# Another order for the first 900 of 2,700 tasks of a recurrence and an MLP on one core

## The chip, the cores and the metric

The kernel runs on one core of a Trainium2 chip. The core has five engines with a queue each: TensorE (PE, matrix products, with weight loads shown apart as PEld), VectorE (DVE), ScalarE (ACT), GpSimd (POOL) and SyncE (SP), which here issues all transfers between main memory and the core. An engine works through its queue strictly in order; engines wait for one another by semaphores. Products are written to PSUM, which VectorE and ScalarE read; everything else lies in SBUF, which GpSimd reads too. The metric is device time of one execution in microseconds (us), less is better.

## The reference

Two blocks in a row. The first is a recurrence over 768 time steps for 4 x 8 heads of width 40, with a 40 x 40 state per head; its output is laid out as 3,072 tokens of 320 channels and goes through an MLP with 2,048 hidden units:

```python
for t in range(S):
    y[:, :, t] = np.einsum('bhd,bhde->bhe', rt, state)
    Sa = np.einsum('bhde,bhe->bhd', state, at)
    state_decay = state * wt[:, :, None, :] - np.einsum('bhd,bhe->bhde', Sa, bt)
    state = state_decay + np.einsum('bhd,bhe->bhde', vt, kt)
...
x = np.ascontiguousarray(attn_out.transpose(0, 2, 1, 3)).reshape(B * S, H * D)
h = x @ w_in
g = h * (1.0 / (1.0 + np.exp(-1.702 * h)))
return (g @ w_out).astype(np.float32)
```

All inputs and outputs are float32.

## The kernel before

**Tiling.** Time is cut into 12 chunks of 64 steps. A unit i is one chunk c = i // 2 for one pair p = i % 2 of batches, with 16 heads; there are 24 units. Within a unit the recurrence is written as matrix products: scores of the 64 steps with one another (N from a and b, A from a and k, RV from r and v), a triangular inverse, and products with the state that the unit two before it left behind. Each chunk's result then passes through the MLP, 256 tokens at a time.

**The steps of a unit**, in the order of their chain:

- `logarithm` (L521) and `decay` (L538): the logarithm of w, its running sums by two products (`cum`, by time, and for the first four units `cumc`, by channel), and exponentials of them: FT and GT, wch, and G.
- `prep` (L613): ahT, bhT and khT are a, b and k times FT or GT; kh and bh are k and b by time, times G. The scores RV and A are products, masked while they are copied out.
- `inverse` (L662): the score N, then five levels. For the first four units (`plain_level`, L765) a level is a product on PE out of which one engine copies the next PT (called PV here) and VectorE transposes the next EX. Then come ES, Tc, the products Q and T21, and T. `preset` (L402) puts ones into a tile beforehand. In this text L0, L2, L4, L6 and L8 are the levels of unit 0, L1 to L9 (odd) those of unit 1, L10 to L18 (even) those of unit 2, and L11 to L19 (odd) those of unit 3.
- `solve` (L844): from unit 2 on the state is scaled (zr), turned (zT) and read (rz); B0 and B1 are products and sums, X is T times B, M is X masked, y is a product of RV, kh, M and bh. Out of y come the new state zraw and the unit's output, which `decayed` (L956) multiplies by FT into x. `part_with` (L967) stores x in main memory, and `get_back` (L973) loads it transposed as xT.
- `mlp` (L983): once both units of a chunk are in xT, 40 tasks `up`, four of GELU, 16 of `down`, and the stores.

A number behind a name is the unit's: N0 is the score N of unit 0, x1 the output of unit 1. In the profile, tiles go by the names in the code: EX<-ps_level is the transpose of a level, PT<-ps_level its copy.

**The weights** come as 64-bit pieces: eight of 1,280 columns, each loaded in four quarters (`weight`, L431), then treated by ScalarE (rebased), VectorE (bounded, shifted, rounded) and GpSimd (joined). Raw pieces go to few places, so that piece 5 is loaded where piece 0 was and has to wait until GpSimd has joined piece 0.

**The order.** `Plan.add` (L65) collects 2,700 tasks with what each reads, writes and needs room for; buffers have one to four slots (L280), so that for instance the load of b2 waits until N0 has read b0. The order is written out by hand, as one text, ORDER (L107), and `Plan.listed` (L89) reads it:

```python
e = next(e for e in ENGINES if ENGINES[e] in one)
n, bank = one.split(ENGINES[e])
t = self.tasks[int(n)]
...
t.engine, t.bank = e, int(bank or 0)
```

So `104a1` is task 104 on ScalarE (p is PE, a ScalarE, d VectorE, g GpSimd, s the transfers that SP issues), with the pair of PSUM banks 1 (there are four pairs, 0 to 3). The tasks are issued in that order (L1054), and so each engine's queue has it. Some tasks may run on either of two or three engines, and the letter decides. All products have line L300, as they go through one helper.

Of the kernel before, what the change touches and what calls it, by code (L numbers as in the profile page):

```python
# [111 lines left out]
279d 63s 280g 119p3 277s 171d1 36s 44s 120d3 343s 125d3 278g 124d3 29d 126p2 170a1 123a3 30d 172p1 122a3 127a2 121a 31d 128p2  # L112
54s 173a1 287a 288p0 289a0 129d2 32g 174d1 134p3 147s 37a 290d0 175p2 135d3 180a2 146s 178a2 275s 176d2 136p1 179a2 479s 38d
181a2 45s 39d 177a 282g 291d 91s 138a1 182p0 188p3 281d 183a0 186p2 139d 137a1 283p0 187a2 184p1 189a3 40d 276s 292p2 46a
284d0 41g 285p3 185d1 344s 148a 286d3 190p0 293a2 294d2 334p1 335p3 357a 140s 191d0 268g 336a3 315d 192p2 47d 337a1 348d 316p0
194a2 295p3 349d 61s 317a0 195g 60s 347s 358p1 296a3 62s 297d3 360d1 318a0 298p3 271a 361d 319p0 338g 300d3 196s 193a2 320a0
346s 355p2 385d 270s 48d 299a3 362p0 356d2 351g 301p3 363a0 364d0 350g 269s 141s 386p2 197s 302d3 365p0 387a2 352g 359a1 303d3
388a2 323p1 367d0 366a0 321p3 49d 324a1 304p2 322a3 478s 325d1 50g 353p0 309a2 470p3 354d0 209p1 307a2 210p1 310a2 305d2 211p1
308a2 272d 198p0 341a 199p0 72s 212p1 70s 64a 200p0 340s 368p2 52s 342d 339s 69s 201p0 369a2 202p0 370d2 203p0 471a 213p1 65d
214p1 389p2 66d 472a3 483g 204p0 390a2 560s 371p3 67d 306a 53s 215p1 71s 482s 216p1 372a3 217p1 476a 220p2 373d3 68g 218p1  # L120
221p2 477d 219a1 205p0 222p2 206p0 223p2 224p2 207p0 55a 311p3 225p2 79s 312d3 80s 226p2 208a0 58d 313p1 374p3 314d1 227p2 56d
379a3 228p2 229p2 57d 326p0 230a2 59g 393p1 327d0 378a3 391p2 394a1 375d3 231p0 558s 392d2 376a 232p0 233p0 395d1 559s 81s 73a
78s 234p0 480s 381p2 235p0 328p1 481s 382a2 74d 377a3 485d 380a3 236p0 75d 492a 242p2 486d 243p2 82a 76d 484d 77g 383p3 237p0
384d3 244p2 329d1 330d1 488p3 473d 238p0 531d 245p2 487g 246p2 489d3 85d 532p1 239p0 533a1 396p3 331d 332s 474s 475s 534a1
240p0 247p2 397d3 562s 241a0 535p1 83d 490p3 536a1 84d 398p0 572a 491d3 86g 550p1 555s 561s 253p3 399d0 551a 333s 400d0 254p3
401d 402s 554s 255p3 552a1 564d 493p0 705s 556a 567g 570p1 403s 494d0 248p2 563d 566g 249p2 495d0 498d 256p3 571d1 565g 250a2
496a0 251d2 252s 696p1 497g 557d 539p0 537p2 704s 257p3 538a2 540d0 258p3 553d 611d 697a 499d 573p2 784s 700s 259p3 576a2
574d2 710d 260p3 541d0 575d2 404p0 578d 261a3 577g 405p0 579d 698a1 568p2 711g 500p1 406p0 569d2 501a1 407p0 262d3 263s 708s
580p2 702a 502d1 408p0 582d2 409p0 503d 410p0 583d 504a 612p3 411p0 584g 613d3 412p0 614d3 413p0 505p1 709d 414a0 426p3 506d1
427p3 428p3 507d1 429p3 699d 581d2 430p3 615p1 785s 706s 701s 703d 431p3 616a1 585p0 432p3 508d 586a0 433p3 587d0 434p3 509a  # L130
588d 435p3 589d 448p2 436a3 510p1 590p0 511a1 449p2 592d0 591a0 512d1 415p3 513d 416p3 593d 514a 417p3 594g 418p3 515p0 419p3
516a0 517d0 595p1 518d 420p3 596a1 597d1 421p3 598d 422p3 519a 599d 423p3 424p3 520p0 425a3 437p1 521d0 438p1 523d0 522g 439p1
524d0 440p1 525d0 441p1 442p1 526d0 527p3 718p0 929s 528a3 443p1 719d0 787s 444p1 720d0 529p3 445p1 721d0 446p1 530d3 600p0
723d 447a1 542p3 722d 724g 603d0 605a0 619p1 604d0 543d3 450p2 620a1 606d0 544p3 621d1 601d0 602d 617p1 707s 546d3 451p2 618a1
783s 712d 547g 713d 607p0 725p1 608a0 452p2 609p0 453p2 548s 610d0 932s 454p2 727d1 726d1 622p0 728d 545d3 729a 775p1 455p2
623d0 780s 776a 549s 756d 730p3 624p0 456d2 457d2 731d3 458s 459p2 777a1 778g 732d3 786s 788g 781a 779s 626d0 460p2 625d0 627g
733d 795p1 835d 734a 461p2 735p3 791g 462p2 628s 736a3 796d1 737d3 716p0 792g 738d 463p2 782d 739g 1011s 920p1 757p3 925s
464p2 717d0 758a3 629s 759a3 790d 465p2 740p0 789d 466p2 741a0 742d0 921a 797p3 467d2 760p0 1008s 468d2 800a3 923d 652p2 469s
761d0 922a1 653p2 926a 930s 798d3 714p1 799d3 654p2 924s 802d 801g 655p2 934d 803a 656p2 836p0 657p2 715d1 658p2 659p2 837d0
762p3 838d0 927d 660p2 763a3 661p2 764p1 662a2 743d 630p0 744d 928s 631p0 632p0 765d1 804p3 766d1 633p0 805a3 806d3 634p0 807d  # L140
635p0 808a 745p2 636p0 748d2 637p0 749d2 839p1 933g 750d2 638p0 840a1 1009s 751d2 639p0 809p3 746d2 935g 640a0 641p1 810d3
642p1 793p2 747a 811d3 674p0 812d 794d2 813a 752p3 643p1 753a3 814p2 644p1 815a2 816d2 754p3 645p1 755d3 646p1 817d 647p1 818a
767p2 841p3 768d2 648p1 842a3 649p1 819p2 650p1 820a2 821d2 675p0 769p3 822d 651a1 823d 771d3 931s 770d3 772g 824p2 936d 676p0
827a2 828a2 942p1 829a2 677p0 1153s 830a2 937d 945a1 773s 663p3 825d2 664p3 943d1 1156s 826a 665p3 944d1 999p2 947d 946g 666p3
1000a 1004s 980d 940p1 948g 667p3 941d1 668p3 774s 669p3 670p3 831p1 671p3 1001a2 1002d 1003s 832d1 672p3 1005a 1013d 678p0
673a3 1006d 833p2 843p1 679p0 834d2 1007s 844d1 938p2 845d1 680p0 939d2 846p3 681p0 847d3 949p1 1012g 682d0 848p2 950a1 683d0
1014d 684s 685p3 849d2 1015g 1010s 850d2 1021p0 1016g 951d1 686p3 1024a0 1232s 851d 1235s 981p2 687p3 982a2 952d 852s 1022d0
983a2 953g 1144p1 1023d0 688p3 1026d 1145a 1149s 1025d 1027g 984p2 1059d 689p3 1154s 954p0 853s 985a2 1147g 690p3 1158d 1148s
955a0 956d0 986p2 1146a1 957d 1150a 691p3 958d 987a2 1151d 988p0 692p3 989a0 1152s 990d0 959p1 693a3 865p2 960a1 694d3 866p2
961d1 867p2 695s 962d 868p2 963d 1028p0 869p2 1029a0 1030d0 870p2 1031d 1157g 871p2 1159d 1032a 1060p3 872p2 873p2 1061a3  # L150
# [987 lines left out]
```

## Time and profile before

| what | us |
|---|---|
| median of 3 runs | 677.05 |
| lowest and highest run | 674.52, 680.86 |
| the profiled execution, from its first to its last instruction (span) | 676.5 |
| PE busy in it | 648.5 (96%) |
| VectorE, ScalarE, GpSimd busy | 444.6, 331.6, 175.3 |

The runs' times and the span are taken in different executions; the median lies 0.55 us above the span. A row of a list by time begins with its start and its length, in us from the start of the span, then engine, line, operation, the tiles written and read, shapes, and how many instructions it joins; in brackets stands how long the engine had been idle and what ended that. An SPq row is the issue of a transfer, not the transfer. Busy time of PE is modelled at the ends of products, so 96% busy does not mean 96% of its peak.

### The profile page before, as it was taken

The page shows a single profiled execution, that of the slowest core. Times are in us where ns is not written, and L with a number is a line of the kernel's source. Part 1 is how long each engine was busy: PE and PEld are TensorE (multiplying, and loading weights), DVE is VectorE, ACT ScalarE, POOL GpSimd, SP SyncE. Part 2 cuts the span into 40 slices and gives each one's busy share as a digit, 9 for nine tenths or more (in the row PEclk, how much of TensorE's full clock was granted, in tenths as well). Part 3 has the DMA queues.
Part 4 walks back from the last instruction along what each step waited for, and adds up shares of the span by engine and source line. Part 5 has one row for each costly group of instructions (what it writes and reads, how often), then busy time and mean ns, then how long its engine had stood idle before and what let it go on. Part 6 is the DMA issues. An engine that isn't in the chain of part 4 may idle for free.

```text
span 676.5 us, 42217 instructions
## 1 busy us (share of the span) xinstructions
PE 648.5 (96%) x19488; PEld 553.4 (82%) x19488; DVE 444.6 (66%) x908; ACT 331.6 (49%) x710; POOL 175.3 (26%) x204
## 2 busy tenths in 40 slices
PE   5768999999999999999999999999999999999997
PEld 5657887987998987788888888798888798798785
DVE  4786787777867667767776587768656766675001
ACT  4676755534564655664545445455454354252110
POOL 6344244224123123123123211322412421300000
PEclk9899999999999999999999999999999999999999
DMA  7983736315314314432404413513412411200200
GB/s 230 300 289 94 232 107 187 103 43 154 108 47 149 93 58 117 121 108 72 118 22 132 141 34 109 156 33 108 140 39 71 122 53 54 61 14 15 61 12 20
DMA packets 35313, 69.74 MB, mean 103 GB/s; under 512 B 5440, under 2 KB 14656, under 8 KB 35136
## 3 DMA queue, kind: packets, MB, share of 16 engines
q1 hardware_dynamic: 35136, 67.03, 32.6%
q8 instruction: 153, 2.51, 1.5%
q14 instruction: 24, 0.20, 0.1%
HBM read 59.15 MB, written 7.86 MB: 99 GB/s over the span
## 4 chain that ended last, share of the span: by engine, by line
PE 93%; DMA 2%; DVE 2%; issue 1%; ACT 1%; DVEq 0%; SPq 0%; ACTq 0%
PE ps_up L300 31%; PE ps_down L300 30%; PE ps_level L300 9%; PE ps_y L300 5%; PE ps_B L300 5%; PE ps_X L300 2%; PE ps_N L300 2%; PE ps_rz L300 2%; PE ps_RV L300 2%; PE ps_A L300 2%; PE ps_zT L300 1%; DMA ak<-in_ak 1%; PE ps_cum L300 1%; PE ps_T L300 1%; DMA b<-in_b 1%
## 5 line engine op out<-in xcount | busy, mean ns | idle before, releaser
L300 PE MATMUL ps_up<-xT_all,w_sb 64*64 64x256 f32 x3840 | 251.0, 377 | 0.8 <-issue 0.4
L300 PE MATMUL ps_down<-w_sb,g 64*64 64x320 f32 x3072 | 237.0, 430 | 0.2 <-ACT zr L877 0.2
L300 PEld LDWEIGHTS ps_up<-xT_all,w_sb 64*64 64x64 f32 x3840 | 170.1, 133 | 15.9 <-issue 1.5
L300 PEld LDWEIGHTS ps_down<-w_sb,g 64*64 64x64 f32 x3072 | 128.0, 133 | 42.8 <-ACT zr L877 0.4
L996 ACT ACTIVATE g<-ps_up 128x1024 f32<-128x1024 f32 x48 | 49.2, 1024 | 45.4 <-PE ps_up L300 45.0
L715 POOL TENSOR_TENSOR EX<-ES,quads 128x512 f32<-128x512 f32 x29 | 38.3, 1322 | 112.7 <-DVE ES L708 74.9
L300 PEld LDWEIGHTS ps_level<-W,EX 64*64 64x64 f32 x2560 | 57.8, 134 | 6.7 <-DVE T L838 0.5
L758 ACT COPY W<-ps_level 128x512 f32<-128x512 f32 (+1 forms) x56 | 29.5, 527 | 67.7 <-PE ps_level L300 65.7
L760 DVE TENSOR_TENSOR E<-two,ps_level 128x256 f32<-128x256 f32 x80 | 33.1, 415 | 34.2 <-ACT W L758 30.1
L300 PE MATMUL ps_level<-W,EX 64*64 64x64 f32 (+1 forms) x2560 | 55.4, 217 | 0.1
L713 ACT ACTIVATE EX<-ES,quads 128x256 f32<-128x256 f32 x80 | 36.3, 501 | 31.0 <-DVE ES L708 30.3
L619 POOL TENSOR_TENSOR ak<-ak,FT 128x512 f32<-128x512 f32 x16 | 20.9, 1305 | 76.6 <-DMA ak<-in_ak 53.4
L708 DVE STREAM_TRANSPOSE ES<-E 128x256 f32<-128x256 f32 x80 | 35.3, 443 | 4.4
L300 PE MATMUL ps_level<-PT,EX 64*64 64x64 f32 (+2 forms) x1280 | 32.8, 235 | 5.1 <-DVE EX L729 3.7
L300 PEld LDWEIGHTS ps_level<-PT,EX 64*64 64x64 f32 x1280 | 30.8, 139 | 8.3 <-DVE EX L729 4.2
L300 PE MATMUL ps_y<-M,bh 64*64 64x104 f32 (+1 forms) x768 | 35.6, 250 | 0.7 <-DVE M L915 0.4
L300 PE MATMUL ps_y<-RV,kh 64*64 64x104 f32 (+1 forms) x768 | 35.6, 251 | 0.0
L899 ACT COPY B<-ps_B 128x416 f32<-128x416 f32 (+1 forms) x34 | 16.6, 492 | 33.4 <-PE ps_B L300 33.2
L300 PEld LDWEIGHTS ps_y<-RV,kh 64*64 64x64 f32 x768 | 28.3, 137 | 2.6 <-DVE M L915 0.5
L689 DVE COPY_PREDICATED PT<-within,ps_N 128x256 f32<-128x256 uint32 x40 | 17.8, 444 | 18.5 <-ACT P L697 13.5
L915 DVE TENSOR_TENSOR M<-ps_X,later 128x832 f32<-128x832 f32 (+1 forms) x24 | 23.8, 993 | 8.3 <-PE ps_X L300 8.1
L300 PE MATMUL ps_B<-RV,A 64*64 64x104 f32 (+1 forms) x768 | 27.9, 252 | 1.1 <-issue 1.1
(131 smaller groups left out, 1088.2 us busy)
## 6 DMA issues: line engine op xcount, KB each, us to landing
ak<-in_ak SPq DMA_DIRECT2D x48, 160.0 KB
rv<-in_rv SPq DMA_DIRECT2D x48, 160.0 KB
time<-in_time SPq DMA_DIRECT2D x24, 320.0 KB
xT_all<-x_dram SPq DMA_DIRECT2D x48, 160.0 KB
wc<-in_wc SPq DMA_DIRECT2D x20, 264.0 KB
logw<-in_w SPq DMA_DIRECT2D x24, 160.0 KB
RV<-in_v SPq DMA_DIRECT2D x24, 160.0 KB
b<-in_b SPq DMA_DIRECT2D x48, 80.0 KB
```

The source lines that it names most:

```text
L300: nc.tensor.matmul(o, lhsT, rhs, start=start, stop=True, skip_group_check=True)
L619: plan.add(R, {"DVE": 690.0, "POOL": 1270.0, "sbuf": True}, lambda t: of(t.engine).tensor_mul(ahT(), ahT(), FT_of(i)), reads=T("ak", "FT") ...
L689: plan.add(R, dve(256), lambda t, n=n: nc.vector.copy_predicated(tiles_of(at(E0_t, i)), every(within_of(n), [128, 2, 4, 32]), blocks(psum( ...
L708: plan.add(rank, dve(256), lambda t: nc.vector.transpose(ES(n), source(t)), writes=[key("ES", n, 6)], **reads)
L713: nc.scalar.activation(dst[:, :, h], ES(n), ACT.Copy, scale=quads[:, h, :1])
L715: of(t.engine).tensor_mul(dst, ES(n).unsqueeze(2).to_broadcast([128, 8, 2, 32]), quads.unsqueeze(1).to_broadcast([128, 8, 2, 32]))
L758: plan.add(rank, any2(512 - 8 * past), lambda t: copy(t.engine)(tiles_of(W(n + 1))[:, :, :, past:], blocks(psum(t, ""), 64)[:, :, :, past: ...
L760: plan.add(rank, dve(256), lambda t: nc.vector.tensor_sub(tiles_of(E(n + 1)), every(two32, [128, 2, 4, 32]), blocks(psum(t, ""), 64)[:, :, ...
L899: plan.add(R, any2(4 * wide), lambda t: copy(t.engine)(dst(), some(psum(t, "")[:, :, :208])), writes=[("Bv", i)] if x and c > 0 else T("B" ...
L915: plan.add(R + 1, dve(8 * wide), lambda t: nc.vector.tensor_tensor(M_of(i)[:, :, :wide].rearrange("p (j b) n -> p b j n", b=2), some(psum( ...
L996: plan.add(-45, {"ACT": 1030.0, "table": "gelu"}, lambda t: nc.scalar.activation(g_of(c * NQ + q).rearrange("p m r n -> p r m n"), psum(t, ...
```

## The change

Only the text ORDER is changed, and nothing that it orders. The first 899 entries are the same 899 tasks in another sequence; 93 of them are on another engine. VectorE has 259 of them instead of 252, GpSimd 55 instead of 50, ScalarE 154 instead of 166; PE keeps 305 and SP 126. From the 900th entry on, task and engine are the same at every place, and the pairs of PSUM banks are renamed throughout: 0 is now 3, 1 is 0, 3 is 1, 2 stays. The start of both texts, where what the prediction speaks of stands:

```diff
-0s 5s 7s 8s 9s 3a 6s 87p0 88p1 24s 89a1 1s 2s 12s 102a 95d 100p2 90a0 93d 158a 101d2 98p3 96g 10s 94d 17s 97g 16s 99d3 103p1
-4a 11s 132p0 104a1 105d1 142p2 26s 143p3 133a0 106d 130p1 14s 144a3 13s 107p0 15s 18s 151g 108a0 109d0 51s 131a1 110p3 27s
-149g 150d 111a3 112d3 159p0 156p1 145a2 161d0 160a0 152g 113p3 345s 92a 162d 25s 153d 114a3 163p2 42s 115d3 34s 19a 274s 264p0
-165d2 265p3 164a2 22d 266a3 166p2 20d 273s 21d 33s 43s 167a2 154p3 168d2 23g 35s 28a 157d1 116p2 155d3 169p1 117a2 118d2 267a0
...
+0s 158a 3a 87p3 6s 88p2 89a2 94d 5s 93d 102a 103p0 9s 7s 95d 1s 105d0 104d0 100p1 8s 101d1 4a 10s 98p2 99d2 90a3 96g 97g
+16s 274s 143p0 106d 142p3 144a0 132p2 145a3 107p1 15s 11s 108a1 130p3 131a3 17s 18s 14s 109d1 152g 149d 150d 151d 133a2
+153g 2s 110p0 159p1 161d1 12s 111a0 112d0 162d 154p2 155d2 160a1 19a 113p3 25s 163p1 22d 27s 92a 265p0 347s 165d1 114a3
+156p2 115d3 13s 273s 20d 164a1 166p1 26s 21d 167a1 157d2 23g 264p2 116p3 266a0 24s 117a3 168d1 118d3 267a2 169p1 279d
+33s 345s 170d1 119p2 60s 120d2 171d1 28a 287a 278g 122a2 124d2 29d 126p0 127a0 288p3 34s 36s 35s 172p1 344s 280g 289a3
+125a2 31d 123a2 121a 37a 128p0 91s 30d 129d0 32g 45s 173d1 174d1 134p2 175p0 178a0 181a0 277s 179a0 135d2 290d3 38d
+136p2 180a0 343s 138a2 276s 39d 139g 176d0 148a 275s 182p0 291d 188p3 183d0 186p1 184p0 137d2 177a 185d0 283p2 140s
+189a3 284d2 187a1 51s 268g 335p3 190p1 281g 292p2 44s 282g 334p0 191d1 340s 336a3 62s 357a 192p1 294d2 315d 348g 40d 42s
...
```

Where to find in it what the prediction speaks of: 6 is the load of b0, 5, 7, 8 and 9 those of a and k, r and v, RV and time of unit 0; 158 and 102 are the preset copies of units 1 and 0, 3 and 4 the logarithms of units 0 and 1; 94, 93 and 95 are bhT0, ahT0 and khT0; 103 is N0; 87 and 142 are cum0 and cum1, 334 is cum3; 90 is G0, 97 is bh0; 107, 110, 116 and 119 are L0, L2, L6 and L8; 134 is X0, 136 is y0, 139 is x0; 190 is X1, 192 is y1, 195 is x1 (further on). 347 is the load of time3 and waits for 152 and 153 (kh1 and bh1); 60 is the quarter of weight 5 and waits for 23 (the joining of weight 0), with 34, 36 and 35 (weight 2), 344 (b3), 91 (logw3), 277 (time2) and 343 (a and k of unit 3) behind it; 340 is logw6, 42 and 43 are quarters of weight 3. 279 is bhT2, 278 and 280 are ahT2 and khT2, 288 is N2. The first task `up` is 209; of five products that stood ahead of it, 386 (zT3), 323 (B12), 304 (L18), 353 (A3) and 470 (cum4) now stand behind.

More of the change, by code (lines that the diff above doesn't have):

```diff
@@ L112 @@
[L112 to L139, printed above, removed]
@@ new lines @@
+1929p1 1862d2 1763p3 1863d 1764p3 1930d1 1864g 1956p2 1765p3 1931d1 1957a2 1766p3 1932d 1958a2 1767p3 1933d 1865p0
+1768p3 1868a0 1934p1 1869a0 1769p3 1935d1 1770p3 1870a0 1794p2 1871a0 1936d1 1937d 1771a3 1866d0 1772p1 1938d 1867g
+1959p0 1773p1 1960a0 2129s 1939p3 1774p1 1940a3 1941d3 1775p1 1942d 1872p0 1776p1 1943d 1873a0 1777p1 2062p3 1778p1
+2065a3 2063d3 2273s 1874p0 1779p1 1875d0 1780p1 2064d3 1781p1 2067d 1887p0 1782a1 2066d 2068g 1783p3 1888d0 1784p3
+1961p1 1944p0 1962a1 1785p3 1945d0 1889p1 1947d0 1946a 1948d0 1949d0 1786p3 2051s 1950d0 1787p3 1891d1 1963p0 1890d1
@@ L245 @@
+2679p3 2655a2 2656p1 2657p1 2658p1 2659p1 2660p1 2661p1 2662p1 2663p1 2664p1 2665p1 2680p3 2666a1 2667p0 2668p0 2669p0
+2670p0 2671p0 2672p0 2673p0 2674p0 2675p0 2676p0 2681p3 2677a0 2682p3 2683p3 2684p3 2685p3 2689p2 2686d3 2687d3 2690p2
+2688s 2691p2 2692p2 2693p2 2694p2 2695p2 2696p2 2697d2 2698d2 2699s
 """
```

233 lines of the change are left out of this document (128 added, 105 removed).

## The prediction

> **What bounds the kernel now.** I read the page's busy picture first, then the busy time by stretch, then PE's waits, then the list in order of time. From the page, in 40 slices of 16.9 us:
>
> ```profile
> PE   5768999999999999999999999999999999999997
> ```
>
> PE is full from the fifth slice on. By stretch:
>
> ```profile
> 0.00:10.00 10.00, 4.14 (x104) 3.60 (x104) 5.28 (x10) 4.14 (x13) 7.92 (x41) 1.00 0.66 193
> 10.00:20.00 10.00, 7.00 (x204) 6.62 (x208) 4.20 (x6) 4.74 (x15) 4.24 (x4) 0.98 0.94 299
> 20.00:30.00 10.00, 7.67 (x283) 6.83 (x281) 7.61 (x12) 7.92 (x18) 2.94 (x2) 0.85 0.82 269
> 30.00:40.00 10.00, 6.64 (x277) 5.51 (x268) 9.37 (x16) 6.51 (x18) 5.97 (x4) 1.00 0.99 327
> 40.00:50.00 10.00, 6.33 (x259) 5.50 (x260) 8.14 (x17) 7.20 (x19) 4.45 (x4) 1.00 0.88 285
> 50.00:60.00 10.00, 8.30 (x333) 8.00 (x336) 5.83 (x9) 6.50 (x18) 4.75 (x8) 0.83 0.23 71
> 60.00:70.00 10.00, 8.24 (x317) 6.85 (x313) 7.41 (x14) 6.34 (x19) 2.96 (x1) 1.00 0.49 138
> 70.00:80.00 10.00, 9.19 (x237) 8.71 (x238) 7.24 (x9) 7.60 (x15) 3.40 (x2) 1.00 0.70 228
> 80.00:600.00 520.00, 519.33 (x15969) 442.34 (x15964) 369.40 (x770) 265.94 (x556) 138.68 (x142) 1.00 0.32 96
> 600.00:676.50 76.50, 71.70 (x1555) 59.50 (x1546) 20.07 (x53) 14.76 (x25) 0.00 (x0) 0.99 0.09 24
> ```
>
> After the stretch and its length come PE, its weight loads, VectorE, ScalarE and GpSimd (busy, instructions), then clock, DMA share and GB/s: from 10 to 50 us the transfer engines are nearly full. Up to 80 us PE is busy 57.5 us, so idle 22.5; in the next 520 us it is idle 0.7; at the end 4.8, which the change leaves alone. Both orders issue the same products. So the change can only win idle time of the first 80 us, and what it wins there reaches the end one for one, as PE is full behind it. Two stretches have a lowered clock: 0.02 and 0.15 of 10 us, and 0.17 of 10 us, are 3.4 us at half rate each, 1.7 us of work lost each. PE can't start before 3.7 us (below). So the most that can be won is 22.5 - 3.7 + 3.4, some 22 us. PE's waits in the first 230 us (total, times, longest):
>
> ```profile
> PE ps_level L300 <- DVE EX L729: 3.7, 3, 1.7
> PE ps_cum L300 <- POOL logw L367: 3.7, 1, 3.7
> PE ps_cum L300 <- issue: 2.1, 1, 2.1
> PE ps_B L300 <- issue: 1.1, 1, 1.1
> ```
>
> No single wait rules: many steps of the first units' chains are late by about 1 us each, and PE stops twice for "issue", with nothing to wait for.
>
> **The change part by part.** It moves 899 tasks in the list and 93 of them to another engine (VectorE 7 more, GpSimd 5 more, ScalarE 12 fewer). Behind these the list is the same but for the names of PSUM pairs (0 to 3, 1 to 0, 3 to 1), which costs nothing: the users of a pair follow each other as before. I walk the new list by hand to the first product of the MLP, with durations of this profile, 0.05 us from an engine to PE and 0.12 from PE to a reader.
>
> *Start.* b0 is loaded second instead of sixth, and N0 is PE's third task.
>
> ```profile
> 0.81 0.41 SPq L492 DMA_DIRECT2D logw<-in_w  x1
> 3.06 0.47 ACT L526 ACTIVATE logw<-logw 128x320 f32<-128x320 f32 x1 [0.98 <-DMA logw<-in_w]
> 4.39 0.73 SPq L503 DMA_DIRECT2D b<-in_b  x2
> 5.98 0.67 ACT L565 ACTIVATE GT<-ps_cumc 128x256 f32<-128x256 f32 x2
> 10.25 0.78 DVE L621 SCALAR_TENSOR_TENSOR b<-b,GT 128x512 f32<-128x512 f32 x1 [0.29 <-DMA b<-in_b]
> 11.29 1.14 PE L300 MATMUL ps_N<-b,ak 40*64 40x64 f32 x32 [1.30 <-DVE b L621]
> ```
>
> Before, N0 waits for b0 although GT is there at 6.65. Now ScalarE's preset copy stands ahead of the first logarithm (+0.3), so GT is there at 6.95; two products of 0.7 on VectorE; N0 at 8.5, 2.8 earlier. Most of that is lost again: VectorE has five pieces of some 0.7 before the first transpose is done (13.65), and cum1 waits for GpSimd's bh0 (13.05), since G0 now stands behind the second logarithm. L0 starts at 14.2 instead of 14.95.
>
> *Levels of units 0 and 1.* The list in order of time:
>
> ```profile
> 14.95 1.43 PE L300 MATMUL ps_level<-PT,EX 64*64 64x96 f32 x32
> 17.55 0.72 DVE L729 STREAM_TRANSPOSE EX<-ps_level 128x512 f32<-128x512 f32 x1 [2.90 <-ACT PT L792]
> 18.32 0.89 PE L300 MATMUL ps_level<-PT,EX 64*64 64x96 f32 x32 [1.71 <-DVE EX L729]
> 29.19 0.89 PE L300 MATMUL ps_level<-PT,EX 64*64 64x96 f32 x32 [0.76 <-DVE EX L729]
> 37.91 0.94 PE L300 MATMUL ps_X<-B,T 64*64 64x104 f32 x32 [1.17 <-DVE T L838]
> ```
>
> The transpose starts when ScalarE's copy out of the same PSUM pair ends, not beside it: two readers of a pair go one after the other, in list order. I keep that, so a level is 1.1 of PE, 0.8 of copy and 0.72 of transpose in a row. It gives L2 at 17.3 (18.32 before), L6 at 27.2 (29.19), L8 at 30.2, X0 at 36.15 (37.91), and x0, now on GpSimd for 1.7 instead of VectorE for 0.9, at 42.5, some 1.9 earlier. So the gain by 42 us is about 2.
>
> *Unit 1 to the MLP.* Rows that price it:
>
> ```profile
> 50.21 0.51 PE L300 MATMUL ps_cum<-logw,edges 64*64 64x160 f32 x3 [2.13 <-issue]
> 51.50 0.38 PE L300 MATMUL ps_y<-RV,kh 64*64 64x104 f32 x2
> 54.98 1.70 POOL L961 TENSOR_TENSOR x<-zr,FT 128x128 f32<-128x128 f32 x4 [6.60 <-ACT zr L953]
> 56.70 0.68 SPq L971 DMA_DIRECT2D x_dram<-x  x2
> 58.84 2.90 SPq L975 DMA_DIRECT2D xT_all<-x_dram  x4
> 67.55 1.89 PE L300 MATMUL ps_up<-xT_all,w_sb 64*64 64x256 f32 x29
> ```
>
> X1 comes at 44.05 after VectorE's T1 at 43.4, cum3 at 45.6 after GpSimd's kh2 and bh2, y1 at 46.1 instead of 51.5: 2.1 of these 5.4 are the "issue" stop, which the walk does not have. Four exponentials, zraw1 and y1's copy on ScalarE, then x1 on GpSimd at 50.5 (before 54.98), stores at 52.3, the two loads of xT issued by 56.3 and, by the 2.2 us from logw0's issue to its reader, there at 58.5. PE's own work ahead (L14, B02, L11, L16, L13) ends at 58.9. First up at 58.8. But five products that stood before it now stand behind it:
>
> ```profile
> 61.75 0.54 PE L300 MATMUL ps_zT<-ident,zr 40*40 40x40 f32 x32
> 63.34 0.59 PE L300 MATMUL ps_B<-RV,A 64*64 64x104 f32 x16
> 66.13 0.63 PE L300 MATMUL ps_level<-PT,EX 64*64 64x32 f32 x32
> 66.81 0.66 PE L300 MATMUL ps_A<-ak 40*64 40x64 f32 x32
> 67.28 0.47 PE L300 MATMUL ps_cum<-logw,edges 64*64 64x160 f32 x8
> ```
>
> From start to start they hold PE for some 0.35, 0.75, 0.7, 0.45 and 0.27, together 2.5. So 58.8 stands for 61.3, against 67.55: the walk wins 6.2.
>
> *SP's queue.* time3 is issued 20th instead of 48th and waits for GpSimd's kh1 and bh1 (20.3): RV1 and ak2 behind it land by 25, their readers come at 26.3 and 29.3. A quarter of weight 5 waits for GpSimd's joining of weight 0 (29.3), with weight 2, b3, logw3, time2 and ak3 queued behind it: at 0.3 MB/us (rates of 269 to 327 GB/s above) logw3 lands at 35 and time2 at 37, wanted at 40.7 and 42.7. logw6 waits for cum3, the last of weight 3 behind it lands at 49, wanted at 50.4. All hidden, with 1.4 us or more in hand; each price is one for one beyond that.
>
> *VectorE beside GpSimd.*
>
> ```profile
> 26.17 0.82 DVE L451 TENSOR_SCALAR w_sb<-w_sb 128x1280 f32<-128x1280 f32 x1
> 33.80 1.26 POOL L619 TENSOR_TENSOR ak<-ak,FT 128x512 f32<-128x512 f32 x1
> 34.01 1.74 DVE L451 TENSOR_SCALAR w_sb<-w_sb 128x1280 f32<-128x1280 f32 x1
> ```
>
> The same operation takes 1.74 when it starts inside GpSimd's product and ends 0.7 after that product. The new list starts that one at 33.15, after GpSimd's second product of unit 2 (31.9): 0.9 of VectorE time, in the walk already. [...]
>
> *Sum.* The walk has no "issue" stops and a full clock. The two large stops are 3.2 us together; the instructions are as many, so I keep half, 1.6. The two half-rate spells are 3.4 of lost work; closer work makes one less likely, and part of it falls into waits: I keep 1.1. 6.2 - 1.6 - 1.1 = 3.5 us won. Both gone: 6.2; both as before: -0.4. A slip of 0.05 at each of some 50 hand-overs is 2.5 more either way. From 58.8 to the end of the moved part I find one stop of 0.4 (L18, behind a transpose on VectorE that ends at 63.6), and of the 93 moves to other engines most lie here, under a full PE: nothing either way. VectorE's slack covers them (369 of 520 us busy); without it a late copy costs PE one for one. The profiled execution's 676.5 would become 673.0; the median of the runs lies 0.55 above it, so 673.5.
>
> **The rivals.**
> *All of it comes, and the stops with it.* No "issue" stop, no half-rate spell and a little less idling among the ups: 7.5 won, 669.5. For it: nothing in the walk needs them. Against: as many instructions have to be brought in, in less time.
> *It moves the waits only.* Units 2 and 3 have the same chain of levels, and the round trip of x1 through DRAM (56.7 to 61.7 in issue alone) is not shortened. If y1 comes no earlier than x1's other conditions allow, the up stage starts for PE where it did: 677. For it: the walk has won only 2 by 42 us.
> *Slower: more half-rate spells.* The spells follow a stretch with PE idle for about half (1.7 of it before 18.32, 2.1 before 50.21). In the walk PE is idle up to N0 at 8.5 and thin from 33 to 36. Each spell costs up to 1.7; four more cancel the walk's 6.2, eight more give 677 + 8 x 1.7 - 6.2 = 684.5. Against: the busy share before the ups rises, as the same work takes less time. [...]
>
> **How the numbers follow.** Forecast 0.50, all of it 0.25, waits only 0.12, slower 0.13. A measurement of this kernel can tell about 1% (6.8 us) from no change. Faster by more than that is the second case, 0.25; the first and third lie within, 0.62; slower 0.13. The range takes the second case with its slips (668) and half of the way to the slower one (681). The likeliest case alone would span 670.5 to 677.5.
>
> **What would show it.** Right: N0's first product near 8.5, L6 near 27, X0 near 36, y1 near 46 to 48, the first up near 59 to 61; PE idle in the first 80 us down from 22.5 to about 19. Wrong: "issue" stops of 2 us in the compressed part, three or more half-rate spells, SP held at weight 5 past 34 us, or PE idle beyond 1 us between 80 and 600 us.

## The result and the profile after

The changed kernel is slower, by 0.7 to 1.5%. In the first comparison it takes 683.3 us (median of 15 runs, 679.45 to 687.34) against 678.95 (15 runs), a ratio of 1.0072 with a 95% interval from 1.0048 to 1.0096. It was measured twice more, on other occasions: 691.32 against 680.74 us, 1.0153 (1.0110 to 1.0196), and 688.89 against 681.96, 1.0112 (1.0068 to 1.0155). So the loss is 4 to 11 us. The forecast was 673.5, in a range from 668 to 681. Ratios here compare fast runs alone, and so does the median of experiment 7, where two of 12 runs (692.24 and 695.08 us) were slow.

The profiled execution has a span of 681.5 us, 5.0 more than before. The products have line L307 now, as the text ORDER is seven lines longer. First the busy picture of the page, then the busy time by stretch, with the columns that the prediction names:

```profile
PE   5688999999999999999999999999999999999997
```

```profile
0.00:10.00 10.00, 2.91 (x72) 2.56 (x72) 5.67 (x11) 3.82 (x12) 7.66 (x40) 1.00 0.62 159
10.00:20.00 10.00, 7.53 (x216) 6.79 (x216) 4.57 (x9) 4.22 (x14) 1.70 (x2) 1.00 0.92 282
20.00:30.00 10.00, 7.43 (x337) 6.86 (x336) 8.20 (x14) 7.26 (x18) 4.71 (x3) 1.00 0.82 242
30.00:40.00 10.00, 6.62 (x228) 5.59 (x220) 8.98 (x14) 6.57 (x16) 6.28 (x4) 0.83 0.89 303
40.00:50.00 10.00, 8.01 (x349) 7.27 (x346) 8.70 (x15) 7.24 (x25) 4.80 (x8) 1.00 0.50 149
50.00:60.00 10.00, 7.18 (x278) 6.69 (x271) 6.63 (x9) 4.09 (x7) 6.70 (x7) 0.86 0.91 282
60.00:70.00 10.00, 9.46 (x306) 7.62 (x302) 8.42 (x17) 6.46 (x10) 2.92 (x1) 0.97 0.67 200
70.00:80.00 10.00, 10.00 (x284) 9.24 (x287) 6.11 (x10) 7.99 (x20) 4.30 (x3) 1.00 0.72 224
80.00:600.00 520.00, 516.77 (x15773) 432.96 (x15767) 366.36 (x764) 256.88 (x545) 136.94 (x143) 1.00 0.32 95
600.00:681.50 81.50, 76.45 (x1700) 74.43 (x1692) 22.24 (x57) 17.90 (x30) 1.08 (x1) 1.00 0.09 24
```

Up to 80 us PE is busy 59.1 us, 1.6 more than before: this execution did win there. Between 80 and 600 us it is idle 3.2 us, where it was 0.7. But busy time doesn't show the whole: PE is busy 652.4 us in all, 3.9 more than before, with the same 19,488 products. Part of its waiting hides in the modelled ends of products.

So a second measure is needed. The start-to-start times of PE's 1,080 tasks are compared with the median of the same kind of task in the run before (0.43 us for `up`, 1.08 for `down`, 0.47 for a level, and so on). The time by which a task starts later than the sum of these medians ahead of it is PE's lost time. At the first task that starts behind each of four points of time, in us, with traces of the experiments below:

| trace | by 80 us | by 230 us | by 600 us | by 660 us |
|---|---|---|---|---|
| before | 29.9 | 31.4 | 32.8 | 30.8 |
| before, pairs renamed | 32.9 | 34.0 | 35.8 | 33.8 |
| changed, first trace | 27.0 | 34.2 | 37.0 | 35.6 |
| changed, second trace | 33.5 | 40.9 | 44.0 | 43.5 |
| changed, third trace | 30.9 | 37.1 | 41.3 | 40.0 |

The first trace of the changed kernel is 2.9 us ahead at 80 us, 2.8 behind at 230 and 4.8 behind at 660. Behind 80 us the list before loses 1.5 and 1.1 us up to 230; the changed one loses 7.2, 7.4 and 6.2. In the first 80 us its three traces differ by 6.5 us. These are two things to explain: the loss behind 80 us, and why the lead does not hold.

Eight of PE's waits in the first 230 us of the changed kernel (total, times, longest), its first trace:

```profile
PE ps_level L307 <- issue: 3.5, 5, 1.4
PE ps_N L307 <- DVE ak L626: 2.7, 1, 2.7
PE ps_level L307 <- DVE EX L736: 2.6, 3, 1.3
PE ps_cum L307 <- issue: 0.9, 1, 0.9
PE ps_level L307 <- ACT EX L720: 0.6, 1, 0.6
PE ps_up L307 <- DMA xT_all<-x_dram: 0.3, 1, 0.3
PE ps_Q L307 <- ACT Tc L812: 0.3, 1, 0.3
PE ps_B L307 <- ACT G L598: 0.3, 1, 0.3
```

The first four lie ahead of 125 us, the last four are new waits behind 80 us. In the list before, PE's waits from 90 to 230 us are no more than these:

```profile
PE ps_up L300 <- PE ps_rz L300: 0.2, 1, 0.2
PE ps_up L300 <- DVE B L902: 0.2, 1, 0.2
```

One of the new waits from the list in order of time:

```profile
140.84 0.64 ACT L812 COPY Tc<-ps_level 32x64 f32<-32x64 f32 x3
141.54 0.46 PE L307 MATMUL ps_Q<-ES,P 64*64 64x64 f32 x16 [0.32 <-ACT Tc L812]
```

The products Q4 wait for the four copies Tc, which the new list gives to ScalarE where VectorE had them. The idle time shown is 0.32 us; by the start-to-start times the stop costs 0.54. Three more of this kind follow: the level L33 at 184.97 (for EX on ScalarE, behind a GELU; 0.73), B0 of unit 7 at 203.65 (for G on ScalarE; 0.51) and an `up` behind Q7 at 200.96 (0.25).

### The profile page after: what moved, and what is told of

Read it like the earlier page. It is cut to its first block, busy times and chain, and to the rows that moved or that the text cites. A ratio compares the mean times of both kernels' runs of the same rounds, so it can differ in the third digit from the quotient of the medians.

```text
span 681.5 us, 42192 instructions
## 1 busy us (share of the span) xinstructions
PE 652.4 (96%) x19488; PEld 560.0 (82%) x19488; DVE 445.9 (65%) x913; ACT 322.4 (47%) x694; POOL 177.1 (26%) x209
## 3 DMA queue, kind: packets, MB, share of 16 engines
q1 hardware_dynamic: 35136, 67.03, 32.9%
## 4 chain that ended last, share of the span: by engine, by line
PE 88%; DVE 4%; ACT 3%; DMA 2%; issue 2%; SPq 1%; DVEq 0%; ACTq 0%
PE ps_down L307 28%; PE ps_up L307 28%; PE ps_level L307 9%; PE ps_y L307 5%; PE ps_B L307 5%; PE ps_X L307 3%; PE ps_N L307 2%; PE ps_A L307 2%; PE ps_RV L307 1%; PE ps_rz L307 1%; PE ps_zT L307 1%; PE ps_Q L307 1%; DMA rv<-in_rv 1%; PE ps_cum L307 1%; PE ps_T L307 1%
## 5 line engine op out<-in xcount | busy, mean ns | idle before, releaser
L307 PE MATMUL ps_up<-xT_all,w_sb 64*64 64x256 f32 x3840 | 252.1, 377 | 0.7 <-DMA xT_all<-x_dram 0.3
L307 PE MATMUL ps_down<-w_sb,g 64*64 64x320 f32 x3072 | 239.7, 430 | 0.6 <-issue 0.4
L307 PEld LDWEIGHTS ps_up<-xT_all,w_sb 64*64 64x64 f32 x3840 | 170.4, 133 | 18.7 <-issue 1.2
L307 PEld LDWEIGHTS ps_down<-w_sb,g 64*64 64x64 f32 x3072 | 138.9, 133 | 34.6 <-issue 1.4
L722 POOL TENSOR_TENSOR EX<-ES,quads 128x512 f32<-128x512 f32 x32 | 41.9, 1311 | 137.8 <-DVE ES L715 92.1
L307 PEld LDWEIGHTS ps_level<-W,EX 64*64 64x64 f32 x2560 | 58.3, 134 | 8.1 <-ACT EX L720 1.6
L307 PE MATMUL ps_level<-W,EX 64*64 64x64 f32 (+1 forms) x2560 | 56.9, 218 | 0.7 <-ACT EX L720 0.6
L765 ACT COPY W<-ps_level 128x512 f32<-128x512 f32 (+1 forms) x52 | 27.6, 531 | 61.9 <-PE ps_level L307 55.7
L767 DVE TENSOR_TENSOR E<-two,ps_level 128x256 f32<-128x256 f32 x80 | 33.1, 414 | 24.4 <-ACT W L765 18.9
L720 ACT ACTIVATE EX<-ES,quads 128x256 f32<-128x256 f32 x74 | 33.6, 501 | 31.6 <-DVE ES L715 31.0
L307 PEld LDWEIGHTS ps_level<-PT,EX 64*64 64x64 f32 x1280 | 32.1, 141 | 12.1 <-issue 4.1
L307 PE MATMUL ps_level<-PT,EX 64*64 64x64 f32 (+2 forms) x1280 | 34.7, 237 | 7.4 <-issue 3.4
L307 PE MATMUL ps_y<-M,bh 64*64 64x104 f32 (+1 forms) x768 | 34.8, 247 | 0.3 <-issue 0.3
L307 PE MATMUL ps_y<-RV,kh 64*64 64x104 f32 (+1 forms) x768 | 34.9, 247 | 0.2 <-DVE M L922 0.2
L634 POOL TENSOR_TENSOR kh<-time,G 128x320 f32<-128x320 f32 x20 | 18.4, 919 | 57.0 <-PE ps_y L307 32.6
L307 PEld LDWEIGHTS ps_y<-RV,kh 64*64 64x64 f32 x768 | 28.1, 133 | 2.5 <-DVE M L922 0.4
L307 PEld LDWEIGHTS ps_B<-RV,A 64*64 64x64 f32 x768 | 25.3, 137 | 4.7 <-ACT G L598 0.8
```

What stands on the lines that cost most here:

```text
L307: nc.tensor.matmul(o, lhsT, rhs, start=start, stop=True, skip_group_check=True)
L634: plan.add(R + 4, {"POOL": 870.0, "DVE": 490.0, "sbuf": True}, lambda t, n=n, dst=dst: of(t.engine).tensor_mul(dst(i)[:, :, :D], by_head(t ...
L720: nc.scalar.activation(dst[:, :, h], ES(n), ACT.Copy, scale=quads[:, h, :1])
L722: of(t.engine).tensor_mul(dst, ES(n).unsqueeze(2).to_broadcast([128, 8, 2, 32]), quads.unsqueeze(1).to_broadcast([128, 8, 2, 32]))
L765: plan.add(rank, any2(512 - 8 * past), lambda t: copy(t.engine)(tiles_of(W(n + 1))[:, :, :, past:], blocks(psum(t, ""), 64)[:, :, :, past: ...
L767: plan.add(rank, dve(256), lambda t: nc.vector.tensor_sub(tiles_of(E(n + 1)), every(two32, [128, 2, 4, 32]), blocks(psum(t, ""), 64)[:, :, ...
```

## The experiments

**1 and 2: half of the change each.** Theory A says that the head of the new list (its first 320 entries, about 80 us) wins, and that the new sequence behind it loses. Experiment 1 has the new head and the old rest, experiment 2 the old head and the new rest. Eight tasks differ between the two heads; they stand at the seam, here that of experiment 1 against the changed list.

```diff
 ... 226p1 58d 227p1
-228p1 56d 229p1 339s 372a2 231p2 311p3 230a1 57d 232p2 ...
+72s 339s 560s 482s 372a2 476a 477d 219a0 311p3 79s 312d3 ...
```

> The first 320 entries of the changed list (the first 80 us) with their engines, then all other tasks in the sequence and on the engines of the list before. Summed over the start-to-start times of PE's tasks, the changed kernel is 2.9 us ahead of the one before at 80 us and 2.8 us behind at 230 us. Theory A (late readers: the loss belongs to the new sequence behind entry 320, where PE stops a dozen times for 0.1 to 1.0 us because a copy or transfer comes late): the lead of 2.9 stays, some 676 us against 679. Rival B (borrowed: the early start of the MLP uses up products that would fill PE later, so the lead is given back whichever sequence follows): 679 to 683 us, with PE idle again between 90 and 230 us.

> The first 320 entries of the list before, then all other tasks in the sequence and on the engines of the changed list. Theory A: no lead at 80 us and the stops of the new sequence behind it, 679 + 4 to 6 = 683 to 685 us. Rival B: nothing was borrowed, so PE does not run out of products: 679 us, within 1 us.

The old head with the new rest takes 686.85 us against 680.04, ratio 1.0088 (1.0059 to 1.0117): 6.8 us slower, a little more than Theory A's 4 to 6. PE loses 31.3 us by 80 us, as with the old head, and 37.9 by 230: the 6.6 us in between are those of the changed kernel (7.2), with stops of 0.54, 0.73, 0.51 and 0.25 us at the same four products. That half of Theory A holds.

The new head with the old rest takes 685.29 us, ratio 1.0075 (1.0049 to 1.0101): slower, where 676 was expected. It was not a clean cut. From the list in order of time:

```profile
87.99 0.64 ACT L528 ACTIVATE wc<-wc 128x528 f32<-128x528 f32 x1 [4.72 <-DMA wc<-in_wc]
89.89 0.40 DVE L829 TENSOR_TENSOR QT<-ps_Q,quads 128x256 f32<-128x256 f32 x1
90.43 0.66 PE L303 MATMUL ps_T<-QT,Tc 64*64 64x64 f32 x13 [7.13 <-DVE QT L829]
```

At the seam the load of wc6 (339s) and the logarithm that reads it (476a) now stand side by side. ScalarE waits 4.7 us for the load, VectorE's sums wait for ScalarE, and PE 7.1 us for a copy queued behind them on VectorE. This is the seam's price, and it hides what the head is worth.

**3: the new sequence, with the old engines behind entry 320** (71 tasks).

```diff
-526a0 525a0 524a0 523a0 499a3 ...
+526d0 525d0 524d0 523d0 499d3 ...
```

> The changed list in its sequence, but behind entry 320 every task on the engine that it has in the list before (71 tasks). Theory A1 (of theory A: the loss comes of the new engines, for instance the two EX halves on ScalarE behind a GELU of 1.02 us and a table load of 1.28 us before the stop at 184 us): the stops go, 677 us. Theory A2 (of theory A: the loss is in the sequence, which puts readers behind other work on their queue): 683 us or more.

697.62 us against 680.04, ratio 1.0252 (1.0226 to 1.0277): it loses 17.6 us to the kernel before, where the changed kernel loses 4 to 11. PE loses 28.4 us by 80 us and 44.0 by 230. So the new engines are not to blame as such. They belong to the new sequence, which is far worse without them.

**4: the list before with the pairs of PSUM banks renamed.**

```diff
-87p0 88p1 89a1 ... 100p2 ... 98p3
+87p3 88p0 89a0 ... 100p2 ... 98p1
```

> The list before with only the pairs of PSUM banks renamed as in the changed list (0 to 3, 1 to 0, 3 to 1). Both theories expect 679 us, within 0.5 us, and its trace serves as a second one of the sequence before: stops of PE that move between the two traces are chance. If the names matter, it is slower by up to 4 us.

681.32 against 680.04 us, ratio 1.0014 (0.9998 to 1.0031): the names cost nothing that shows. Its trace loses 32.9 us by 80 us instead of 29.9, with 13.7 us at half rate in the first 100 us instead of 6.8. One and the same sequence varies by 3 us there from trace to trace.

**5 and 9: the head alone, with better seams.** In experiment 5 the logarithm 476a and its sums stand some 100 entries later. In experiment 9 the list before keeps its own 320 first tasks, in the new sequence, with the load 339s moved ahead, and is untouched from entry 321 on.

```diff
 experiment 5
-... 372a2 476a 477d 219a0 ... 399d0 551a
+... 372a2 219a0 ... 399d0 476a 477d 551a
 experiment 9
-... 70s 66d ... 372a2 339s 219a0 ...
+... 70s 339s 66d ... 372a2 219a0 ...
```

> As the first experiment (the changed list up to entry 320, the list before behind it), but the logarithm log6 and its sums, which at the seam stood right behind the transfer of wc6 and held ScalarE's queue for 4.7 us (and PE for 7.1), stand some 100 entries later, before the exponentials of unit 5. Theory A (the new head wins 3 us and the new sequence behind it loses them): some 677 us against 680 for the kernel before. Rival B (the win of the head is borrowed and is given back under any sequence): 680 us or more, with PE idle in 0.3 to 1 us pieces between 90 and 230 us.

> The list before, whose first 320 tasks stand in the sequence and on the engines of the changed list (with the transfer of wc6 30 entries ahead of the logarithm that reads it); from the 321st entry on it is the list before, entry by entry. Theory A (the head wins about 3 us, the new sequence behind it loses them and 4 more): 3 us less than the kernel before, and PE loses under 2 us between 80 and 230 us. Rival B (the win of the head is borrowed): no faster than the kernel before, with the lead of the first 80 us gone at 230 us though the list there is the old one.

Experiment 5 takes 685.89 us against 680.74, ratio 1.0068 (1.0038 to 1.0099); experiment 9 takes 689.20 against 681.96, ratio 1.0107 (1.0068 to 1.0146). Both are slower, so Theory A's other half, that the head wins 3 us, is borne out by no run. Rival B is not shown either: what PE loses has other names than a lack of products. In experiment 5 the trace has a stop of 2.5 us for issue at an `up` at 92.7 us and 1.5 us of waiting at cum6, which is the moved logarithm's doing. In experiment 9 PE stops 9.2 us for issue in the first 90 us, and 1.0 for a GELU at the seam. The seams are still not clean, so the times of these two hybrids do not price the head by themselves.

**6 and 12: the changed kernel again.** No edit.

> The changed kernel itself on the same chip as the others, for a comparison in one place and a second trace: 683 to 685 us. Stops of PE that stand at the same product in both of its traces belong to the list; stops that wander belong to chance.

> The changed kernel once more beside the others: 4 to 10 us above the kernel before (it was 4.4 above in the first comparison and 10.6 in the second). The stops of 0.54 us at Q4, 0.73 at L33, 0.51 at B0 of unit 7 and 0.25 behind Q7 stand again at the same products, 2.0 us in all; what stops for issue is at other products than in the first two traces.

The times stand above; experiment 6 missed its 683 to 685 us, and 12 lies in its range. The four stops behind 80 us are at the same products in all three traces: 0.54, 0.55 and 0.54 us at Q4; 0.73, 0.74 and 0.62 at L33; 0.51, 0.52 and 0.51 at B0 of unit 7; 0.25 three times behind Q7. They make up 2 us of each trace's 6 to 7 and belong to the list. The stops for issue wander (1.0 us at L21 at 120 us in the first trace, 1.36 at rz5 at 135 in the second, 0.74 at zT8 at 221 in the third). In the first 80 us they are most of what makes the three traces so unlike; the spells at half rate differ too (6.8, 13.7 and 13.7 us in the first 100). The waits of the second one:

```profile
PE ps_level L307 <- issue: 7.2, 5, 2.5
PE ps_RV L307 <- issue: 2.1, 1, 2.1
PE ps_A L307 <- issue: 1.4, 1, 1.4
PE ps_cum L307 <- issue: 0.7, 1, 0.7
PE ps_up L307 <- issue: 0.4, 1, 0.4
```

Over all traces with every transfer, PE stops for issue in the first 90 us for 4.0, 13.3 and 8.8 us in the changed kernel and for 4.0 to 13.3 in the eight traces with the new head (mean 7.8). In the six with the old head, experiments 8, 10 and 11 below among them, which change nothing before 90 us, it is 4.9 to 7.5 (mean 6.5).

**7: three products of the changed list moved two MLP products back.**

```diff
-439p1 527p0 440p1 528a0 441p1 718p3
+439p1 440p1 441p1 527p0 528a0 718p3
-638p0 766d3 808a 809p2 810d2 639p0 641p3
+638p0 766d3 808a 639p0 641p3 809p2 810d2
-667p0 841p2 668p0 669p0
+667p0 668p0 669p0 841p2
```

> The changed list with three products moved two MLP products back, Q4 (which waits for Tc on ScalarE), the level L33 (which waits for EX on ScalarE) and B0 of unit 7 (which waits for G on ScalarE). Theory A with late readers as the cause: the three stops of 0.54, 0.73 and 0.51 us go, 1.8 us less than the changed kernel. If PE's lost time behind 80 us is for the most part something else (stops for its own instructions, shown as issue), those three go and the total moves by less than 1.8 us.

685.2 us against 691.32 for the changed kernel beside it; the ratio to the kernel before falls from 1.0153 (1.0110 to 1.0196) to 1.0079 (1.0044 to 1.0114). The intervals just touch. The three stops are gone from the trace, and PE loses 4.5 us from 80 to 230 us instead of 6.2 to 7.4. What is left of its waits from 80 to 230 us:

```profile
PE ps_B L303 <- ACT B L902: 0.4, 1, 0.4
PE ps_N L303 <- ACT g L999: 0.3, 1, 0.3
```

Late readers are a cause, then, worth about 2 us by the traces; two smaller ones appeared in their place. The time fell by more than the 1.8 us expected, and the three stops don't account for the rest.

**8 and 10: what an issue stop is.** The list before, with the products `up` of the second chunk (119 to 146 us) cut into four of 64 columns each: the same sums, four times as many instructions. The diff is that of experiment 8; in experiment 10 the loop over j is the outer one.

```diff
-                for r, h in QUARTERS:
-                    mm(ph[HALF[h], r, m * 256:(m + 1) * 256], w_in_sb[...], x[HALF[r]], m == 0 and k == 0)
+                for r, h in QUARTERS:
+                    for j in range(0, 256, 64):
+                        mm(ph[HALF[h], r, m * 256 + j:m * 256 + j + 64], w_in_sb[...],
+                           x[HALF[r], j // 128, j % 128:j % 128 + 64], m == 0 and k == 0 and j == 0)
```

> The list before; each product of the 40 tasks up of the second chunk (119 to 146 us) is cut into four of 64 columns, the same sums in 64 instructions of PE and its weight loads for each task instead of 16. Theory F (PE can't take in instructions faster than 256 in 3.3 to 4.0 us, as the spacing of its instruction transfers shows, and stops for issue where a stretch of small products needs them faster): such a task takes 0.83 to 1.0 us in a run of them instead of 0.69, the time of the levels of the same shape, with issue stops of 6 to 12 us in all in the stretch. Without F: 0.69 us each and no issue stops.

> As the experiment with narrow products, with the four pieces of a column block in the outer place, so that four parts of PE's array take turns as they do in the levels (before, four products in a row used one part, and took 31 ns each with no stop). Theory F (instructions come in at 256 in 3.3 us at most): the levels' pace of 0.69 us for 64 instructions would be 256 in 2.76 us, so in a run of these products PE stops for issue, 0.5 us or more for each 256 instructions, and a task takes 0.83 us or more. Without F: 0.69 us and no issue stops.

Experiment 8 (715.83 us, one run) has one stop for issue from 90 to 230 us, of 0.4, and decides nothing: with four products in a row on one quarter of the array a task of 32 takes 1.15 us in the median, 36 ns a product (not 31, as the expectation of 10 has it), so that 256 instructions take 4.6 us. Busy time by stretch of experiment 8, then of experiment 10 (707.9 us, one run), where the quarters take turns:

```profile
150.00:160.00 10.00, 10.00 (x319) 9.71 (x321) 1.95 (x6) 3.47 (x6) 1.27 (x1) 1.00 0.02 6
160.00:170.00 10.00, 10.00 (x323) 10.00 (x318) 4.08 (x13) 2.20 (x4) 1.26 (x1) 1.00 0.01 3
```

```profile
150.00:160.00 10.00, 6.47 (x397) 5.94 (x390) 4.37 (x14) 2.68 (x5) 1.39 (x2) 1.00 0.02 5
160.00:170.00 10.00, 6.27 (x352) 5.86 (x355) 3.01 (x10) 1.85 (x4) 1.27 (x1) 1.00 0.18 54
```

PE is now busy only 6.4 of 10 us, with the transfer engines nearly idle (0.02 and 0.18). Its waits from 90 to 230 us:

```profile
PE ps_up L300 <- issue: 10.1, 5, 3.6
PE ps_level L300 <- issue: 4.2, 4, 1.4
PE ps_zT L300 <- issue: 2.8, 1, 2.8
PE ps_N L300 <- issue: 1.2, 1, 1.2
PE ps_down L300 <- issue: 0.6, 1, 0.6
```

That is 18.9 us in 12 stops, where the list before has none. Count all that PE's queue holds: products, weight loads and the instructions by which PE waits for semaphores. Then six stops in a row stand behind PE's first 6,593, 6,849, 7,106, 7,361, 7,617 and 7,873 instructions: one at every 256th. The same count settles what the stops for issue are elsewhere. The 16 traces show 171 of them, of 0.15 us or more, and 169 have 193 or 194 instructions more than a multiple of 256 ahead of them. So have all 106 of the first 92 us, with either head, and those behind 80 us that wander from trace to trace. Of PE's 280 waits for an engine or a transfer, none has. So a stop for issue is the end of a block of 256 instructions (but for two, in experiments 3 and 11); which of the blocks end in one varies.

Instructions come as transfers of 16 KB, 256 at a time. The page of the changed kernel counts them (packets, MB, share of the transfer engines' time):

```profile
q8 instruction: 153, 2.51, 1.5%
```

153 packets of 16,384 bytes for 38,976 products and weight loads and PE's few others. In the 16 traces the closest two of these packets are 3.26 to 3.38 us apart, and the median distance is 4.0 to 4.2. Theory F holds for a run of dense blocks: in experiment 10, 16 blocks take less than 3.3 us from their first instruction to their last, and 14 of them end in a stop. A single dense block need not end in one: in the trace before it is 3 of 8, and its other 5 stops end longer blocks, of 3.4 to 5.0 us, so that there the next block came late by more than PE's own pace explains. The price that the expectations name is wrong. 0.69 us is the time of a level with 40 products; one with 32 takes 0.46, as the cut tasks do where nothing stops them (0.47 in the median), which is 256 instructions in some 1.9 us. With the stops a task takes 0.77 in the mean, not 0.83 or more.

**11: more transfers on the list before.** 53 more transfers of 320 KB between 90 and 215 us, which nothing reads.

```diff
     for n, t in enumerate(tasks):
         t.fn(t)
+        if t.engine == "SP" and 380 <= n < 900:
+            nc.sync.dma_start(more[n % 8][:], time_d[0, 0:128])
```

> The list before; behind each of SP's 53 transfers from entry 380 to 900 (90 to 215 us) stands one more, 320 KB from one place of main memory to another that nothing reads. Theory G (PE's instructions come by the same transfer engines as the data, late where these are full, and PE then stops for issue): the list before, which stops for issue 0.4 us or less there, now stops for 2 us or more in pieces of 0.3 to 2.5 us, at products that are in no dense run; 2 to 8 us slower. Without G: no issue stops, and PE waits at most for data that come late.

706.02 against 681.96 us, ratio 1.0355 (1.0317 to 1.0393). PE's waits from 90 to 230 us:

```profile
PE ps_up L300 <- DMA xT_all<-x_dram: 7.2, 1, 7.2
PE ps_up L300 <- DVE ES L708: 3.2, 1, 3.2
PE ps_y L300 <- issue: 0.7, 1, 0.7
PE ps_up L300 <- issue: 0.5, 1, 0.5
PE ps_down L300 <- issue: 0.2, 1, 0.2
```

Three stops for issue where there were none, but 1.4 us and not 2, and the kernel is 24 us slower, not 2 to 8; most of the loss is data that come late. The effect that Theory G names shows better in the packets themselves. From 90 to 215 us they start 1.56 us in the mean behind PE's first instruction of a block, 11 of 26 more than 1.8 us behind it; in the two traces of this list without the added transfers it is 0.82 and 0.69 us, with 2 and 1 of 30. In the traces before, after and of experiments 1, 2, 4, 5, 6 and 7, of the 4th to the 120th instruction packet of each, those that start more than 100 instructions late (PE has by then begun over 100 more than 256 for each packet) are 0.3% where the transfer engines were under 0.2 busy in the 3 us before, 0.6% at 0.4 to 0.6, 5.8% at 0.6 to 0.8 and 24.5% above 0.8.

**13 and 14: both lists with fewer transfers.** Part of the loads is left out: the last three weight pieces and rv, RV and time of units 2 to 6.

```diff
-nc.sync.dma_start(raw()[:, some], src[:, some])
+n < 5 and nc.sync.dma_start(raw()[:, some], src[:, some])
-for p in rows:
+for p in rows if name in ("ak", "b") or not 2 <= i <= 6 else ():
```

> The list before without part of its transfers, for its time alone: the last three weight pieces and rv, RV and time of units 2 to 6 are not loaded (what lies in their places from before is used), some 7 of the 18 to 20 MB of the first 90 us. Theory G (PE's instructions come late because the transfer engines are full of data): the stops of PE for issue in the first 90 us, 4.9 to 7.5 us in the traces with the old head so far, fall to under 3 us. Theory F (256 instructions in 3.3 us at most and some 4 in the mean, data or not, and a head that is a run of small products): they stay at 5 to 7 us.

> The changed list without the same transfers. Theory G: its stops for issue in the first 90 us, 4.0 to 13.3 us so far, fall to under 3 us, and its head is 3 us or more ahead of that of the thin list before at 90 us, as it was forecast; in the end it is within 3 us of it, the new sequence behind 80 us giving the lead back. Theory F: the stops stay at 5 to 9 us, its head is not ahead, and in the end it is 4 to 8 us slower than the thin list before, as with all transfers.

678.02 and 681.24 us against 679.52 for the full kernel before: ratios of 0.9969 (0.9946 to 0.9993) and 1.0028 (1.0007 to 1.0050), so the changed list loses 3.2 us to the other, a little less than the 4 to 11 with all transfers. PE stops for issue 3.7 us in the first 90 us of the thin list before and 6.0 in the thin changed list. Neither is under 3, so Theory G's figure fails. Theory F's 5 to 9 holds for the new head, and its 5 to 7 fails for the old one. The lost time by 80 us is 28.6 and 26.3, so that the new head leads by 2.3; by 230 us it is 29.8 and 31.6. So in these two traces a lead is there and the rest of the list gives it back; one trace of each can't tell that from the 6 us by which the traces of one list differ.

## Why the prediction was wrong

**The step that failed first** is the last one of the sum: "From 58.8 to the end of the moved part I find one stop of 0.4 ... nothing either way", with "VectorE's slack covers them". It was priced at nothing and costs 5 to 6 us: 6.2 to 7.4 lost from 80 to 230 us instead of 1.1 to 1.5. One of the signs that the prediction gave for being wrong came with it: PE idle 3.2 us between 80 and 600 us, where it said beyond 1. The cover named was VectorE's spare time, which is an average over 520 us. The stops came from ScalarE's queue, where a GELU of 1.02 us, a table load of 1.28 or four copies in a row stand ahead of one copy that PE needs; the prediction did not walk that part of the list. Four such stops are 2 us in each trace, and moving three of them took them away. A second part stands at the ends of blocks: from 80 to 230 us the tasks that hold one exceed their medians by 2.5, 3.8 and 3.3 us in the three traces, against 0.6 and 0.3 in the two of the list before. In this stretch the new sequence has more places where 512 instructions of PE are due in under 7.2 us (8.8% of its positions against 4.9%, by the medians above). That this is why it stops there more often was not tried by itself.

**The win of the head** was forecast at 3.5 us. The first trace has 2.9. Over all traces with every transfer it is 1.2 in the mean (30.1 us lost by 80 us in eight traces with the new head, 27.0 to 33.5; 31.3 in six with the old, 27.8 to 33.9), too little against that spread to be called a win. (In two of the eight this counts a stop that ends just behind 80 us; without these it is 1.8.) The mis-sized term is "I keep half, 1.6" for the issue stops: they measure 4.0 to 13.3 us in the first 90 us. The gain that was to pay for them is small as well. In the first 80 us PE waits for other engines 12.8 us in the mean with either head, for transfers 0.7 us instead of 2.4, and for issue 7.4 instead of 6.5. The argument that the two large stops might be half gone took them for accidents. They stand at ends of blocks, in both lists: the one at cum3 has the same 2,241 instructions ahead of it in 15 of the 16 traces, and lasts 0.4 to 2.1 us.

**The walk by hand** holds in its order and is short in its times. In the first trace:

```profile
8.19 0.44 PE L307 MATMUL ps_N<-b,ak 40*64 40x64 f32 x2 [2.71 <-DVE ak L626]
18.98 0.31 PE L307 MATMUL ps_level<-PT,EX 64*64 64x96 f32 x4 [1.28 <-DVE EX L736]
38.13 0.41 PE L307 MATMUL ps_X<-B,T 64*64 64x104 f32 x8 [1.01 <-DVE T L845]
48.24 0.35 PE L307 MATMUL ps_cum<-logw,edges 64*64 64x160 f32 x2 [0.87 <-issue]
51.27 0.46 POOL L968 TENSOR_TENSOR x<-zr,FT 128x128 f32<-128x128 f32 x1 [0.26 <-ACT zr L960]
52.19 0.30 PE L307 MATMUL ps_level<-PT,EX 64*64 64x96 f32 x2 [1.04 <-issue]
56.64 0.47 PE L307 MATMUL ps_level<-PT,EX 64*64 64x96 f32 x11 [1.43 <-issue]
63.60 0.40 PE L307 MATMUL ps_up<-xT_all,w_sb 64*64 64x256 f32 x4
```

N0 comes at 8.19 (8.5 said), L2 at 18.98 (17.3), X0 at 38.13 (36.15), x1 at 51.27 (50.5), the first `up` at 63.60 (58.8; 67.55 before). From L2 to x1 the walk is 0.8 to 2.0 us early. L2 and X0 even come later than in the list before (18.32 and 37.91), so that the 2 us that the walk has won by 42 us are not there; nor are they in the other two traces, with X0 at 40.36 and 39.19. The 4.8 us at the first `up` are for the most part three stops for issue of 0.87, 1.04 and 1.43 and a half-rate spell at 57.1, worth up to 1.7. Had the 2.7 that the sum kept for both been put into the walk, it would have said 61.5.

**Right:** the names of the pairs (nothing that shows in the time); SP at weight 5, held to 30.4 us and harmless, as in the first trace PE waits for no transfer between 12 and 229 us; and VectorE beside GpSimd, where a weight's step (task 29), put behind GpSimd's second product of unit 2, took 0.83 us (at 34.54) instead of 1.74, while bhT2, begun at 30.53 inside GpSimd's ahT2 (30.37 to 31.64), took 1.67 instead of 0.68, the median of its 24. The idle time of the first 80 us was to fall from 22.5 to some 19 us and fell to 20.9 in the first trace; in the other two, with 55.8 and 57.8 us busy, it is 24.2 and 22.2.

**The rivals.** "Slower" came true, by another mechanism than the one given. Half-rate spells in the first 100 us are 14.5 us in the mean with the new head and 13.1 with the old (each 6.8 to 23.9), which is 0.7 us of work. "It moves the waits only" is refuted in its place, as the first `up` does come 4.0 us earlier in that trace, of which 2.5 are the five products that now stand behind it. But it names the outcome: the waits changed their cause.

**Open:** the changed kernel loses 1 to 3 us more than the list before between 230 and 600 us, where both lists are the same but for the names (2.8, 3.1 and 4.2 against 1.4 and 1.8). Stops for issue are 0.7 to 1.2 us there against none, and the tasks that hold the end of a block exceed their medians by 1.9, 1.8 and 3.2 us against 1.0 and 1.0. Why blocks come later there, with the same instructions, is not settled. Nor is what the new head alone is worth in time, as each seam had waits of its own; and no version that does all the work beats the kernel before.

## What to carry to other kernels

When an order is changed, walk the list behind the last product that you care about too, for every engine whose copies PE waits for: PE, busy 519.3 of 520 us in the list before, had no slack, and spare time in the mean does not say that a queue is free at the moment (ScalarE was busy 256.9 of these 520 us in the new list, and four stops for its late copies cost PE 2 us). Before forecasting that a denser PE wins, count its instructions against the pace at which they come (here 256 in 3.26 us at the closest, 4.0 to 4.2 in the median); of 16 blocks that took less than 3.3 us from their first instruction to their last, 14 ended in a stop for issue (experiment 10), and time saved on waits can go there. Such stops can be told from others by counting the instructions ahead of them (193 or 194 more than a multiple of 256 at 169 of 171 here, and at none of 280 other waits). Take more than one trace of each version when the forecast is half a per cent: one and the same list varied by 6 us in its first 80.

## What the runs showed of the hardware

PE's instructions come in blocks of 256, the closest 3.26 to 3.38 us apart and 4.0 to 4.2 in the median, and PE stops at a block's end when the next is not there: 12 stops, 18.9 us, in experiment 10, and 169 of the 171 stops for issue in all traces. At those in the traces before and after PE goes on 1.25 to 1.54 us behind the end of a packet of instructions. Blocks start late where the transfer engines are full: 24.5% of them over 100 instructions late above 0.8, 0.3% under 0.2. Half-rate spells of TensorE (a granted clock of 0.50) came singly (3.41 us) and joined (6.83 and 10.24). In the 16 traces 42 of them begin in the first 100 us, each behind 3.41 us in which PE was busy 62% or less; of 37 such windows at full clock with PE busy less than half, 32 were followed by one. Four products of 64 columns in a row on one quarter of the array took 36 ns each (1.15 us for 32, experiment 8), where quarters in turn take 14.5 (0.46 us for 32, the levels).
